# A decode layer pair with its gradients on one core: unread products in TensorE's waits, other staging places, rows issued by SP, one more wq chunk kept

## The chip, the cores and the metric

The kernel runs on one NeuronCore of one Trainium2 chip. The core has five engines with instruction streams of their own: TensorE (PE, matrix products, results only into PSUM), VectorE (DVE), ScalarE (ACT), GpSimd (POOL) and SyncE (SP). SP, ACT and POOL can issue DMA transfers, which all run on the same 16 DMA engines. On chip there are SBUF (128 partitions) and PSUM (8 banks of 128 partitions x 512 fp32). The metric is the device time of one launch in microseconds. Inputs and outputs lie in HBM as the reference has them.

## The reference

One token (a row x of D = 1024 numbers) goes through attention, MLP, attention, MLP, with the same weights both times; then everything is differentiated. In short:

```
A(x): q = x @ wq (1024 -> 32 heads x 128); k, v = the last W = 4096 rows of each of 4 cache heads
      p = softmax(q k^T / sqrt(128)); o = p v; result o @ wo (4096 -> 1024)
B(x): h = x @ w1 + b1 (1024 -> 3584); result (h * tanh(softplus(h))) @ w2 (3584 -> 1024)
x = x + A(layernorm(x)); x = x + B(layernorm(x)); x = x + A(...); x = x + B(...)
outputs: x, and the gradients of x, k_cache, v_cache, wq, wo, w1, b1, w2 for a given grad_out
```

All arrays are bf16. A weight's gradient is the sum over the two layers of an outer product of two vectors, so it is a matrix product over only 2 rows that yields 7.3 to 8.4 MB of output. The cache gradients have 4 heads x 32768 rows x 128; only the last 4096 rows of a head are not zero, so 2 x 29.4 MB of zeros have to be written.

## The kernel before

**Order.** The order of the instructions on every engine is the order in which the Python code emits them; there is no scheduler. The stages follow one another: forward A0, B0, A1, B1 (`attn_fwd`, `mlp_fwd`), backward B1 (`dn_b1`), A1 (`attn_bwd(1, ...)`), the w2 stage (L895 to 900: the second MLP's output and the gradient towards B0's hidden layer), the W1 stage (`dn_b0`, L759), A0 (`attn_bwd(0, ...)`, L1034), and a last stage `work(10000)` (L1042) that finishes the weight gradients.

**Loads.** KT and VS (the used part of the caches, 4 MB each) and W1 stay in SBUF. All chunks of wq, wo and w2 go through a ring of 8 slots of 1 MB (`Ring`, L38). A list of wanted chunks in fixed order (L249 to 265) is worked off by `pump`: whenever a slot is released, SP issues the next load into it. wq is wanted four times (forward and backward of two layers), wo three times (the forward chunks of layer 1 are still in the ring for the backward), w2 twice. `KEEP_Q` (L246) names the wq chunks that layer 0's forward leaves in the ring for layer 1's forward; `KEEP_Q2` (L247) those that layer 1's backward leaves for layer 0's. A kept chunk is not loaded again, and holds its slot meanwhile. In the backward of layer 1 half of every wq chunk is transposed in place; a chunk kept there is not transposed again (`turned_q`).

**Products of one row.** A matrix times one vector is done in two ways side by side. Half of a chunk is multiplied on VectorE (`rowdot`, L392: 1024 columns against the vector, summed). The other half is transposed on PE 128 x 128 at a time into one of three PSUM buffers (`big`), copied back by ACT (`turned`, L417), and then used as the stationary side of products with one column (`mv`, L431), which add up in the PSUM bank TP. `later` (L405) delays these so that PE transposes ahead. A chunk's slot is released after its last product.

**Norms.** `ln_fwd` (L337) and `ln_bwd` (L367) sum over partitions with one small product into the bank SM, which VectorE reads. SM also receives the small sums of the softmax.

**Zeros.** The 56 zero jobs of 1 MB each are issued by POOL in portions: `zeros(n, after)` (L235) first copies one element of `after` on POOL, so that the portion starts when `after` is there, and then issues n jobs. The portions stand at fixed places of the program.

**Weight gradients.** Their outer products need both layers' vectors as rows. `rowize` (L876) and `rowize_f` (L744) transpose a vector's columns on PE, ACT copies the result to SBUF, and two DMAs issued by ACT bring it into `ROWS`. Three of these six run inside `dn_b0`, plus `rowize_f`; two more and the one for GA in the first step of A0's backward (`do1`, L994). One tile of a gradient is a product of 2 rows into 128 x 512 (`unit_dw`, L919), evicted to bf16 by VectorE or ACT, whichever has less work planned (`evac`). Eight tiles (seven for w1) fill one of the staging places in `stage_free`, and SP stores it. Four staging places lie in W1, which is not needed any more after `dn_b0` (L873); in `dq1` (L1010) the eight of VS and KT are put behind them, and for the last stage those of the ring behind these. `work(n)` (L979) emits n tiles, taken in turn from several gradients; it is called between the chunks of A0's backward (`do1`, `dp1`, `dq1`, `dn1`), 53 tiles in all, and then for the remaining 251.

Of the kernel before, what the change touches and what calls it, by code (L numbers as in the profile page):

```python
# [83 lines left out]
def kernel(  # L84
# [62 lines left out]
    SM = psum.tile([P, 512], FP32, name="SM")  # L147
# [98 lines left out]
    KEEP_Q = (6, 7)  # L246
    KEEP_Q2 = (5, 6, 7)  # L247
# [89 lines left out]
    def ln_fwd(x, st, dst_bf, name):  # L337

        nc.tensor.matmul(SM[:, 0:2], lhsT=onesD[:], rhs=st[:], start=True, stop=True)
        mv = tmp([P, 2], FP32, "mv")  # L340
        nc.vector.tensor_copy(mv[:], SM[:, 0:2])
# [12 lines left out]
        nc.scalar.activation(dummy[:, 1:2], dummy[:, 0:1], ACT.Exp)  # L354
        return n32, rstd
# [11 lines left out]
    def ln_bwd(part, n32, rstd, g, name):  # L367
# [12 lines left out]
        nc.tensor.matmul(SM[:, 0:2], lhsT=onesD[:], rhs=st[:], start=True, stop=True)  # L380
        ab = tmp([P, 2], FP32, "ab")
        nc.vector.tensor_copy(ab[:], SM[:, 0:2])
# [19 lines left out]

    lag = deque()
# [46 lines left out]
    def attn_fwd(l, x, st, first, wo_hook, q_hook=None):  # L450
# [19 lines left out]
        nc.gpsimd.tensor_copy(qv[:, 1, :, 1, l, :], qv[:, 0, :, 0, l, :])  # L470
        m64 = [tmp([P, 64], FP32, f"m64{i}") for i in range(2)]
# [20 lines left out]
        nc.tensor.matmul(SM[:, 64:128], lhsT=onesD[0:HQ, :], rhs=dg[:], start=True, stop=True)  # L492
        nm = tmp([P, 64], FP32, "nm")
        nc.vector.tensor_copy(nm[:], SM[:, 64:128])
# [21 lines left out]
        for u in range(2):  # L516
            nc.tensor.matmul(SM[:, 128:160], lhsT=onesD[:], rhs=ssv[:, :, u, :], start=(u == 0), stop=(u == 1))

        rs = tmp([P, HQ], FP32, "rs")
        nc.vector.tensor_scalar(out=rs[:], in0=SM[:, 128:160], scalar1=float(D), scalar2=None, op0=ALU.mult)  # L520
# [178 lines left out]
    def wo_hook1(c):  # L699
        if c == 0:  # L700
            zeros(6, OC[:, 0, 1:2])
# [28 lines left out]
    def dn_b1(g):  # L730
# [11 lines left out]
        return ln_bwd(dnp, sB1["n32"], sB1["rstd"], g, "B1")  # L742

    def rowize_f():  # L744
# [11 lines left out]
    early = [lambda: rowize(OC, HQ, 32, NOFF), lambda: rowize(NA, TD, 0, 0), rowize_f,  # L756
             lambda: rowize(NB, TD, 64, 0), lambda: rowize(AC, TF, 96, NOFF), lambda: rowize(GB, TD, 96, 0)]

    def dn_b0(g):  # L759
        mv_open()  # L760
        for t in range(TD):
            mv(W1[:, t, :], TF, TP[:, t:t + 1], lambda i: DHC[:, i, 0:1], True)
            if t >= 4:
                early.pop()()
        return ln_bwd(None, sB0["n32"], sB0["rstd"], g, "B0")

    def attn_bwd(l, sv, g, wo_key, wq_key, wq_keep, hooks):
# [11 lines left out]
        flush()  # L779
        do_n = from_fours([x.rearrange("p (c k) -> p c k", k=4)[:, :, 2 * h:2 * h + 2]  # L780
# [13 lines left out]
        for i in range(2):  # L794
# [5 lines left out]
            if i == 0:  # L800
                nc.tensor.matmul(SM[:, 192:256], lhsT=onesD[:], rhs=pr[:], start=True, stop=True)
                nc.vector.tensor_copy(sdp[:], SM[:, 192:256])
# [37 lines left out]
        return ln_bwd(dnp, sv["n32"], sv["rstd"], g, name)  # L840
# [35 lines left out]
    def rowize(cols, n, base, off):  # L876
# [6 lines left out]
        for l in range(2):  # L883
            nc.scalar.dma_start(ROWS[base + l:base + l + 1, off:off + n * P].rearrange("o (t p) -> o t p", p=P),  # L884
                                rt[l:2 * n:2, k, :])
# [9 lines left out]
    for c in range(7):  # L895
# [3 lines left out]
        later(lambda c=c: ring.release(("2", 1, c)))  # L899
    flush()  # L900
# [7 lines left out]
    zeros(2, g1)  # L908
# [165 lines left out]
```

## Time and profile before

| what | value |
|---|---|
| time, median of 3 runs | 474.96 us (474.57 to 476.11) |
| profiled execution, its own time | 478.89 us |
| its span | 477.1 us |
| PE busy / DVE busy / ACT busy / POOL busy | 351.7 / 277.9 / 245.3 / 45.2 us |
| mean granted TensorE clock | 0.593 |
| bytes moved by the DMA engines | 183.41 MB, mean 384 GB/s |
| zero jobs on POOL's queue | 56 of 1 MB, 58.7 MB |
| last eviction / end of the span | 457.8 / 477.1 us |

The profile is one execution; times inside it are microseconds from the start of its span, which is 1.8 us shorter than the time of that execution. Busy times of engines overlap and do not add up to the span. A granted clock of 0.5 means that TensorE ran at half speed. The DMA share is the mean busy share of the 16 DMA engines. An entry such as `[1.59 <-DMA W<-W]` behind a row says how long the engine sat idle before it, and what it waited for.

### The profile page before, as it was taken

The numbers are of one execution on the slowest core, as the hardware profiler recorded it, in microseconds if no ns is written. First come the engines' busy times: TensorE is split into PE (matmuls) and PEld (weight loads), VectorE is DVE, ScalarE is ACT, GpSimd is POOL, SyncE is SP. The second block draws the span as 40 slices with busy tenths as digits, with TensorE's granted clock in tenths as the row PEclk, the third lists the DMA queues.
The fourth block names the chain that finished last, engine by engine and source line by source line (L and its number), as shares of the span: only waits on it lengthen the run. The fifth ranks groups of instructions, "written<-read, shape, count | busy, mean of one in ns | idle before, by whom it ended". The sixth has DMA issues, their size and how long they took to land.

```text
span 477.1 us, 13273 instructions
## 1 busy us (share of the span) xinstructions
PE 351.7 (74%) x5841; PEld 268.5 (56%) x5841; DVE 277.9 (58%) x597; ACT 245.3 (51%) x358; POOL 45.2 (9%) x83
## 2 busy tenths in 40 slices
PE   4846345696688895888886976688778689999930
PEld 3746335696588784877876975556456323333300
DVE  4405820561331268896598825466176889999920
ACT  2402001171145296792594633675267589999920
POOL 1000000000043130102201011002302200000000
PEclk9955555555555588797897555555555555555555
DMA  8999999999969999999999999678999999999997
GB/s 337 423 419 419 418 419 418 421 400 383 420 252 394 396 394 406 347 410 368 416 421 366 363 345 414 229 190 325 417 420 415 388 415 413 418 420 414 419 420 306
DMA packets 33992, 183.41 MB, mean 384 GB/s; under 512 B 4217, under 2 KB 4238, under 8 KB 20622
## 3 DMA queue, kind: packets, MB, share of 16 engines
q1 hardware_dynamic: 17280, 123.74, 64.5%
q0 software_dynamic: 15232, 58.72, 31.2%
q8 instruction: 45, 0.74, 0.6%
q10 hardware_dynamic: 1422, 0.10, 0.2%
q14 instruction: 13, 0.11, 0.1%
HBM read 83.90 MB, written 98.58 MB: 382 GB/s over the span
## 4 chain that ended last, share of the span: by engine, by line
PE 46%; DMA 19%; DVE 16%; issue 7%; ACT 6%; ACTq 2%; DVEq 0%; SPq 0%
DVE junk L399 10%; PE BIG L921 8%; PE BIG L421 8%; DMA ring<-in_A_wo_dram 6%; PE SC L921 5%; DMA ring<-in_A_wq_dram 4%; DMA W<-in_B_w_dram 4%; PE BIG L568 3%; ACT ring L282 3%; PE MV L634 3%; DMA out_dram<-W 3%; PE BIG L967 2%; PE TP L433 2%; PE MV L587 2%; ACTq L884 2%
## 5 line engine op out<-in xcount | busy, mean ns | idle before, releaser
L282 ACT COPY ring<-BIG 128x1024 bf16<-128x1024 bf16 x82 | 81.8, 1046 | 38.5 <-PE BIG L421 29.4
L399 DVE CUSTOM_DVE_ANT_0 junk<-ring,SC 128x1024 bf16<-128x1024 bf16 x62 | 75.5, 1217 | 6.1 <-PE SC L305 3.4
L421 PE MATMUL BIG<-ident_bf,ring 128*128 128x128 bf16 x656 | 71.0, 278 | 8.9 <-ACT ring L282 2.4
L921 PE MATMUL BIG<-W 2*128 2x512 bf16 x163 | 68.3, 586 | 7.5 <-ACT W L282 3.2
L421 PEld LDWEIGHTS <-ring 128*128 128x128 bf16 x656 | 57.4, 126 | 22.0 <-issue 21.0
L921 PEld LDWEIGHTS <-W 2*128 2x128 bf16 x240 | 20.2, 101 | 39.9 <-issue 35.3
L243 POOL DMA_DIRECT2D out_dram<-zt x56 | 40.2, 720 | 3.5 <-DMA out_dram<-zt 3.0
L282 ACT COPY KT<-BIG 128x1024 bf16<-128x1024 bf16 x22 | 21.8, 1015 | 31.5 <-PE BIG L568 29.6
L282 ACT CAST W<-BIG 128x512 bf16<-128x512 f32 x55 | 31.2, 595 | 11.5 <-PE BIG L921 9.3
L433 PEld LDWEIGHTS <-ring 128*128 128x128 bf16 x704 | 30.8, 107 | 11.2 <-ACT ring L282 6.3
L921 PE MATMUL SC<-W 2*128 2x512 bf16 x77 | 35.3, 584 | 0.4 <-ACT VS L282 0.4
L282 ACT COPY W<-BIG 128x1024 bf16<-128x1024 bf16 (+2 forms) x33 | 26.5, 908 | 17.2 <-PE BIG L727 14.8
L279 DVE CAST W<-BIG 128x512 bf16<-128x512 f32 x30 | 20.3, 686 | 20.8 <-PE BIG L921 13.4
L539 PE MATMUL MV<-OC,ring 128*128 128x1 bf16 x512 | 16.5, 166 | 13.0 <-DMA ring<-in_A_wo_dram 12.2
L587 PE MATMUL MV<-NB,W 128*128 128x1 bf16 x448 | 16.4, 172 | 10.0 <-DMA W<-in_B_w_dram 6.6
L539 PEld LDWEIGHTS <-ring 128*128 128x128 bf16 x512 | 15.9, 106 | 13.7 <-DMA ring<-in_A_wo_dram 12.8
L461 PE MATMUL MV<-NA,ring 128*128 128x1 bf16 x512 | 15.0, 165 | 10.6 <-DMA ring<-in_A_wq_dram 9.4
L399 DVE CUSTOM_DVE_ANT_0 junk<-ring,DSX 128x1024 bf16<-128x1024 bf16 x18 | 22.0, 1224 | 0.5
L587 PEld LDWEIGHTS <-W 128*128 128x128 bf16 x448 | 16.1, 118 | 10.7 <-DMA W<-in_B_w_dram 7.7
L399 DVE CUSTOM_DVE_ANT_0 junk<-ring,SC,dnp 128x1024 bf16<-128x1024 bf16 x16 | 20.5, 1281 | 0.6
L967 PEld LDWEIGHTS <-W 32*128 32x128 bf16 x128 | 9.6, 101 | 19.9 <-issue 18.3
L461 PEld LDWEIGHTS <-ring 128*128 128x128 bf16 x512 | 14.3, 103 | 11.2 <-DMA ring<-in_A_wq_dram 10.0
(253 smaller groups left out, 593.3 us busy)
## 6 DMA issues: line engine op xcount, KB each, us to landing
out_dram<-zt POOLq DMA_DIRECT2D x56, 1024.0 KB, 13.0
ring<-in_A_wq_dram SPq DMA_DIRECT2D x27, 1024.0 KB
ring<-in_A_wo_dram SPq DMA_DIRECT2D x24, 1024.0 KB
ring<-in_B_w_dram SPq DMA_DIRECT2D x14, 1024.0 KB
out_dram<-W SPq DMA_DIRECT2D x11, 1024.0 KB
W<-in_B_w_dram SPq DMA_DIRECT2D x8, 896.0 KB
out_dram<-KT SPq DMA_DIRECT2D x7, 1024.0 KB
out_dram<-ring SPq DMA_DIRECT2D x7, 1024.0 KB
```

The lines of the kernel that those rows point to most:

```text
L243: nc.gpsimd.dma_start(dst, zt[:, None, :].to_broadcast([P, dst.shape[1], ZC]))
L279: nc.vector.tensor_copy(dst, src)
L282: nc.scalar.copy(dst, src)
L399: nc.vector.tensor_tensor_reduce(out=out, in0=a, in1=vec, scale=1.0, scalar=acc if i else 0.0, op0=ALU.mult, op1=ALU.add, accum_out=acc)
L421: nc.tensor.transpose(b[:, i * P:(i + 1) * P], block(w, i) if block else w[:, i * P:(i + 1) * P], ident_bf[:])
L433: nc.tensor.matmul(out, lhsT=w[:, i * P:(i + 1) * P], rhs=rhs_of(i), start=fresh[0], stop=last and i == n - 1, skip_group_check=True)
L461: nc.tensor.matmul(q_ps[:, h:h + 1], lhsT=ch[:, h * P:(h + 1) * P], rhs=NA[:, t, l:l + 1], start=(t == 0 and h == 0), stop=(t == TD - 1), ...
L539: nc.tensor.matmul(y_ps[:, dd:dd + 1], lhsT=ch[:, tt, dd * P:(dd + 1) * P], rhs=OC[:, h, l:l + 1], start=(h == 0 and dd == 0), stop=(h == ...
L568: nc.tensor.transpose(b[:, i * P:(i + 1) * P], T[:, g, 8 * b8 + i, :], ident_bf[:])
L587: nc.tensor.matmul(h_ps[:, fb:fb + 1], lhsT=f_block(W1[:, t], fb), rhs=NB[:, t, l:l + 1], start=(t == 0 and fb == 0), stop=(t == TD - 1), ...
L921: nc.tensor.matmul(b[:, 0:n], lhsT=ROWS[base:base + 2, lo:lo + P], rhs=ROWS[base:base + 2, ro:ro + n], start=True, stop=True, tile_positio ...
L967: nc.tensor.matmul(b[:, k * 256:(k + 1) * 256], lhsT=RT[32 * g:32 * g + 32, a, tp, :], rhs=YS[32 * g:32 * g + 32, :], start=True, stop=Tru ...
```

## The change

Seven things change together:

1. `warm(n)`: n products of 128 x 512 (the identity as weights, zeros as the moving side) into a PSUM bank WM that nothing reads. 100 of them are emitted: in `from_fours`, before and after the small product of `ln_bwd` (11 and 4 for B1, 8 and 2 for B0, 6 and 4 for A1, none for A0), one per chunk of the w2 stage and of the W1 stage, three at the end of the wo loops, two per chunk of A0's wo and wq loops, six in `dq1`.
2. SM makes room for WM: the small sums go to columns 128 to 384 of TP.
3. `KEEP_Q` gets chunk 5, `KEEP_Q2` chunk 4, so that wq is loaded two chunks less in all.
4. Staging: VS's four places are put in front of the list in `dp1`, KT's four in `dq1`.
5. The row transfers are issued by SP instead of ACT.
6. `rowize_f`, NA and OC are turned to rows right after the norm's product of `ln_bwd` for B0; GB, AC, NB in steps 4 to 6 of the W1 stage; GA stays in `do1`.
7. Zeros: two jobs after the query of layer 1's forward, 5 instead of 6 at wo's first chunk, 3 instead of 2 after g1, two each at c = 2 and c = 5 of A0's wo loop, 4 instead of 5 in `dq1`, 3 instead of 4 at t = 2 of `dn1`; at t = 5 none are left. There are 56 as before.

```diff
-    SM = psum.tile([P, 512], FP32, name="SM")
+    WM = psum.tile([P, 512], FP32, name="WM")
...
-    KEEP_Q = (6, 7)
-    KEEP_Q2 = (5, 6, 7)
+    KEEP_Q = (5, 6, 7)
+    KEEP_Q2 = (4, 5, 6, 7)
...
+        warm(3)
         return TP[:, 480:512]
 
+    def warm(n):
+
+        for _ in range(n):
+            nc.tensor.matmul(WM[:], lhsT=ident_bf[:], rhs=zt[:, 0:512], start=True, stop=True)
...
-    def ln_bwd(part, n32, rstd, g, name):
+    def ln_bwd(part, n32, rstd, g, name, before=0, after=0):
...
-        nc.tensor.matmul(SM[:, 0:2], lhsT=onesD[:], rhs=st[:], start=True, stop=True)
+        warm(before)
+        nc.tensor.matmul(TP[:, 128:130], lhsT=onesD[:], rhs=st[:], start=True, stop=True)
+        while early:
+            early.pop()()
+        warm(after)
         ab = tmp([P, 2], FP32, "ab")
-        nc.vector.tensor_copy(ab[:], SM[:, 0:2])
+        nc.vector.tensor_copy(ab[:], TP[:, 128:130])
...
         nc.gpsimd.tensor_copy(qv[:, 1, :, 1, l, :], qv[:, 0, :, 0, l, :])
+        if not first:
+            zeros(2, QC[:, 0, 8:9])
...
         if c == 0:
-            zeros(6, OC[:, 0, 1:2])
+            zeros(5, OC[:, 0, 1:2])
...
         for l in range(2):
-            nc.scalar.dma_start(ROWS[64 + l:65 + l, NOFF:NOFF + F].rearrange("o (c j) -> o c j", j=512),
+            nc.sync.dma_start(ROWS[64 + l:65 + l, NOFF:NOFF + F].rearrange("o (c j) -> o c j", j=512),
                                 rf[:, 512 * l:512 * l + 512])
...
             mv(W1[:, t, :], TF, TP[:, t:t + 1], lambda i: DHC[:, i, 0:1], True)
-            if t >= 4:
+            warm(1)
+            if t == 4:
+                early.extend(rows)
+            if 4 <= t < 7:
                 early.pop()()
-        return ln_bwd(None, sB0["n32"], sB0["rstd"], g, "B0")
+        return ln_bwd(None, sB0["n32"], sB0["rstd"], g, "B0", 8, 2)
...
         flush()
+        warm(3)
         do_n = from_fours([x.rearrange("p (c k) -> p c k", k=4)[:, :, 2 * h:2 * h + 2]
...
         later(lambda c=c: ring.release(("2", 1, c)))
+        warm(1)
...
+    do1_acc = tmp([P, HQ], FP32, "do32")
+
     def do1(c):
         if c == 0:
             rowize(GA, TD, 32, 0)
-            while early:
-                early.pop()()
             todo[1].append(units_rows(32, HQ, out_5))
...
+        warm(2)
+        if c in (2, 5):
+            zeros(2, do1_acc[:, 4 * c - 4:4 * c - 3])
         if c >= 2:
             work(3)
 
     def dp1():
         zeros(4, tmp([P, 64], FP32, "m641"))
+        stage_free.extendleft(VS[:, g].rearrange("p t d -> p (t d)") for g in range(G))
         work(5)
 
     def dq1():
-
-        for T in (VS, KT):
-            for g in range(G):
-                stage_free.append(T[:, g].rearrange("p t d -> p (t d)"))
+        stage_free.extendleft(KT[:, g].rearrange("p t d -> p (t d)") for g in range(G))
         rowize(DQC, HQ, 0, NOFF)
-        zeros(5, DQC[:, 0, 0:1])
+        zeros(4, DQC[:, 0, 0:1])
+        warm(6)
         work(6)
 
     def dn1(t):
         if t in (2, 5):
-            zeros(4, dnp[:, t:t + 1])
+            zeros(3, dnp[:, t:t + 1])
...
+        warm(2)
         work(3)
```

More of the change, by code (lines that the diff above doesn't have):

```diff
@@ L333, in from_fours @@
             nc.tensor.matmul(TP[:, 480:512], lhsT=spread[:, 3 - k:P + 3 - k], rhs=dm[:, k, :], start=(k == 0), stop=(k == 3))
+        warm(3)
         return TP[:, 480:512]
+    def warm(n):
+        for _ in range(n):
+            nc.tensor.matmul(WM[:], lhsT=ident_bf[:], rhs=zt[:, 0:512], start=True, stop=True)
     def ln_fwd(x, st, dst_bf, name):
-        nc.tensor.matmul(SM[:, 0:2], lhsT=onesD[:], rhs=st[:], start=True, stop=True)
+        nc.tensor.matmul(TP[:, 128:130], lhsT=onesD[:], rhs=st[:], start=True, stop=True)
         mv = tmp([P, 2], FP32, "mv")
-        nc.vector.tensor_copy(mv[:], SM[:, 0:2])
+        nc.vector.tensor_copy(mv[:], TP[:, 128:130])
         nvar = tmp([P, 1], FP32, "nvar")
@@ L379, in ln_bwd @@
                                        accum_out=st[:, 1:2])
-        nc.tensor.matmul(SM[:, 0:2], lhsT=onesD[:], rhs=st[:], start=True, stop=True)
+        warm(before)
+        nc.tensor.matmul(TP[:, 128:130], lhsT=onesD[:], rhs=st[:], start=True, stop=True)
+        while early:
+            early.pop()()
+        warm(after)
         ab = tmp([P, 2], FP32, "ab")
-        nc.vector.tensor_copy(ab[:], SM[:, 0:2])
+        nc.vector.tensor_copy(ab[:], TP[:, 128:130])
         nc.vector.scalar_tensor_tensor(out=t2[:], in0=n32[:], scalar=ab[:, 1:2], in1=dn[:], op0=ALU.mult,
@@ L401, in rowdot @@
         load["D"] += len(vecs) * (n * 1.1e-3 + 0.18)
+    early = []
     lag = deque()
@@ L491, in attn_fwd @@
         nc.vector.tensor_scalar(out=dg[:], in0=id64[:], scalar1=mh[:, 0:1], scalar2=float(D), op0=ALU.mult, op1=ALU.mult)
-        nc.tensor.matmul(SM[:, 64:128], lhsT=onesD[0:HQ, :], rhs=dg[:], start=True, stop=True)
+        nc.tensor.matmul(TP[:, 192:256], lhsT=onesD[0:HQ, :], rhs=dg[:], start=True, stop=True)
         nm = tmp([P, 64], FP32, "nm")
-        nc.vector.tensor_copy(nm[:], SM[:, 64:128])
+        nc.vector.tensor_copy(nm[:], TP[:, 192:256])
         if not first:
@@ L516, in attn_fwd @@
         for u in range(2):
-            nc.tensor.matmul(SM[:, 128:160], lhsT=onesD[:], rhs=ssv[:, :, u, :], start=(u == 0), stop=(u == 1))
+            nc.tensor.matmul(TP[:, 256:288], lhsT=onesD[:], rhs=ssv[:, :, u, :], start=(u == 0), stop=(u == 1))
         rs = tmp([P, HQ], FP32, "rs")
-        nc.vector.tensor_scalar(out=rs[:], in0=SM[:, 128:160], scalar1=float(D), scalar2=None, op0=ALU.mult)
+        nc.vector.tensor_scalar(out=rs[:], in0=TP[:, 256:288], scalar1=float(D), scalar2=None, op0=ALU.mult)
         nc.vector.reciprocal(rs[:], rs[:])
@@ L741, in dn_b1 @@
         flush()
-        return ln_bwd(dnp, sB1["n32"], sB1["rstd"], g, "B1")
+        return ln_bwd(dnp, sB1["n32"], sB1["rstd"], g, "B1", 11, 4)
     def rowize_f():
@@ L752, in rowize_f @@
         for l in range(2):
-            nc.scalar.dma_start(ROWS[64 + l:65 + l, NOFF:NOFF + F].rearrange("o (c j) -> o c j", j=512),
+            nc.sync.dma_start(ROWS[64 + l:65 + l, NOFF:NOFF + F].rearrange("o (c j) -> o c j", j=512),
                                 rf[:, 512 * l:512 * l + 512])
-    early = [lambda: rowize(OC, HQ, 32, NOFF), lambda: rowize(NA, TD, 0, 0), rowize_f,
+    rows = [lambda: rowize(OC, HQ, 32, NOFF), lambda: rowize(NA, TD, 0, 0), rowize_f,
              lambda: rowize(NB, TD, 64, 0), lambda: rowize(AC, TF, 96, NOFF), lambda: rowize(GB, TD, 96, 0)]
@@ L800, in attn_bwd @@
             if i == 0:
-                nc.tensor.matmul(SM[:, 192:256], lhsT=onesD[:], rhs=pr[:], start=True, stop=True)
-                nc.vector.tensor_copy(sdp[:], SM[:, 192:256])
+                nc.tensor.matmul(TP[:, 320:384], lhsT=onesD[:], rhs=pr[:], start=True, stop=True)
+                nc.vector.tensor_copy(sdp[:], TP[:, 320:384])
             s = SC[i].rearrange("p (tp c) -> p tp c", c=64)
@@ L839, in attn_bwd @@
         flush()
-        return ln_bwd(dnp, sv["n32"], sv["rstd"], g, name)
+        return ln_bwd(dnp, sv["n32"], sv["rstd"], g, name, *((6, 4) if l else (0, 0)))
     turned_q = set()
@@ L883, in rowize @@
         for l in range(2):
-            nc.scalar.dma_start(ROWS[base + l:base + l + 1, off:off + n * P].rearrange("o (t p) -> o t p", p=P),
-                                rt[l:2 * n:2, k, :])
+            nc.sync.dma_start(ROWS[base + l:base + l + 1, off:off + n * P].rearrange("o (t p) -> o t p", p=P),
+                              rt[l:2 * n:2, k, :])
     nc.vector.tensor_copy(GB[:, :, 0], g2[:])
@@ L907 @@
     nc.vector.tensor_copy(GA[:, :, 0], g1[:])
-    zeros(2, g1)
+    zeros(3, g1)
     x4 = sb([P, TD], BF16, "x4")
```

## The prediction

> **What bounds the kernel now.** I read the page's slices first, then a table of chosen stretches, then the chain that ended last, then single rows in order of time.
>
> ```profile
> PEclk9955555555555588797897555555555555555555
> DMA  8999999999969999999999999678999999999997
> ```
>
> The DMA engines are busy nearly everywhere and the granted TensorE clock is mostly half. The stretches (PE, PEld, DVE, ACT, POOL busy; then clock, DMA share, GB/s):
>
> ```profile
> 131.00:137.00 6.00, 4.69 (x150) 4.67 (x148) 3.14 (x9) 2.79 (x4) 0.12 (x1) 0.50 0.61 253
> 137.00:150.00 13.00, 12.60 (x301) 12.54 (x301) 1.11 (x2) 6.97 (x7) 4.91 (x7) 0.50 0.87 332
> 190.40:193.80 3.40, 2.15 (x21) 2.06 (x22) 2.03 (x7) 0.12 (x1) 2.19 (x4) 0.50 0.73 298
> 255.00:258.40 3.40, 2.15 (x46) 2.13 (x46) 2.08 (x6) 0.00 (x0) 2.27 (x4) 0.60 0.65 268
> 256.00:281.00 25.00, 22.86 (x473) 22.59 (x474) 17.91 (x33) 14.07 (x14) 2.92 (x6) 0.50 0.96 354
> 281.00:296.00 15.00, 11.14 (x251) 10.00 (x249) 4.13 (x17) 2.08 (x5) 3.34 (x6) 0.50 1.00 383
> 296.00:305.00 9.00, 5.34 (x66) 4.54 (x65) 7.31 (x12) 4.99 (x9) 0.00 (x0) 0.50 0.75 288
> 305.00:328.00 23.00, 18.48 (x195) 12.73 (x196) 12.60 (x22) 18.45 (x27) 0.00 (x0) 0.50 0.71 223
> 384.00:457.80 73.80, 73.00 (x308) 22.59 (x303) 71.17 (x115) 71.61 (x136) 0.00 (x0) 0.50 1.01 417
> 457.80:473.80 16.00, 0.00 (x0) 0.00 (x0) 0.00 (x0) 0.22 (x1) 0.00 (x0) 0.50 1.00 415
> ```
>
> The last two rows decide how everything else counts. The engines finish evicting at 457.8 us (the last store is issued at 458.04), yet the DMA engines stay full for 16 us more: what ends the kernel is the sum of its transfers plus every moment in which the DMA engines had nothing to do. That idle time is 2.3 + 1.7 us at 131 to 150 us, and 2.3 + 6.7 = 9.0 us at 296 to 328 us (length times the share missing from 1); smaller pieces are 0.9 at 190.4 and 1.2 at 255.0. Engine work that ends earlier helps only if it hands transfers over sooner. Why the second hole exists, from the chain of waits:
>
> ```profile
> 289.85 1.18 ACTq L884
> ...
> 301.08 5.00 DMA W<-W
> ...
> 335.47 12.00 DMA out_dram<-W
> ```
>
> and from the rows in order of time:
>
> ```profile
> 306.38 0.82 PE L921 MATMUL BIG<-W 2*128 2x512 bf16 x3 [1.59 <-DMA W<-W]
> ...
> 343.79 0.69 DVE L279 CAST W<-BIG 128x512 bf16<-128x512 f32 x1 [3.99 <-DMA out_dram<-W]
> 347.56 1.29 DVE L279 CAST W<-BIG 128x512 bf16<-128x512 f32 x2 [3.08 <-DMA out_dram<-W]
> ```
>
> ACT spends 286.8 to 302.2 us issuing row transfers; the last lands at 306, and PE, in order, holds its first gradient product (and all behind it) until then. At 343 and 347 VectorE waits for a store to empty one of only four staging slots.
>
> **The change, part by part.** Two sums: the DMA engines', which sets the end, and the engines', which must stay inside the 16 us of slack.
>
> *One more wq chunk kept, twice.* Two loads of 1 MB go. A wq chunk in the stretch of steady loads comes every 2.5 us (PE starts at 24.27, 26.74, 29.23): -5.0 us of transfer. The ring then has one free slot fewer. In the second layer's q stage five loads instead of six go through the same releases, the last still at 110.17 us, so PE gains 0 to 2.5 us; I take 0.7, since after the last landing three kept chunks follow instead of two. In the second case one w2 load moves from before 255 us to after.
>
> *Zeros at other places.* 56 jobs as before (POOL issues each in 0.72 us); 2 go to the second q stage, 4 into the wo loop of layer 0 (c = 2 and 5), 1 more after g1; the last stage loses 4 and others 1 each. The four in the loop are 4.2 MB, 10 us at 417 GB/s, for a hole of 9.0: I take -8.0, bounds 0 (the hole stays) and -9.0. In the first hole 2 go in and 1 goes from the next batch, and one wq load is missing from the stretch: idle there stays about 5; the loads that arrive sooner and the net megabyte give -1.0, bounds 0 and -2.5. At 255 us the chain comes sooner (below) while one load is deferred: -0.8, bounds +1.3 and -1.2. POOL's copies that gate the jobs wait on VectorE; only zeros queue behind them.
>
> *Rate.* 256 to 281 us moves 354 GB/s at a share of 0.96. At 417 it would be 3.8 us shorter, and 281 to 296 us 1.2 (383 GB/s). I take -1.0 between 0 and -5.0, nearer nothing as loads and zeros still mix.
>
> DMA sum: -5.0 - 8.0 - 1.0 - 0.8 - 1.0 = -15.8 us.
>
> *Rows sent by SP.* 16 issues (0.6 to 1.05 us each, 11 us on ACT up to 302) leave ACT. On SP they are queued ahead of the wo loads of chunks 4 to 7; SP is idle then, and chunk 4 is needed some 10 us after chunk 0, so this costs nothing; without that cover up to 11 us. With ACT free, chunks 0 and 1 take about 2 x 2.2 us from 293 and the first product could start near 299 instead of 306: -6.
>
> *Staging first in V's and K's places.* The two waits of 3.99 and 3.08 us go (-7); the six unread products now there cost 1.3 to 2.6: net -5.
>
> *Kept chunk already transposed.* In the last wq loop t = 4 needs no 16 transposes and 2 copies: a period of 2.6 us (that of t = 5 to 7) instead of 3.7: -1.
>
> *100 unread products of 512 columns.* The trace has no such product. Transposes of 128 columns start 0.106 us apart at half clock (16 from 192.58 to 194.28) and 0.055 at full (8 from 201.82 to 202.26); four times that is 0.43 and 0.22 us, so 43 or 22 us on PE in all. The nearest product with 512 columns, L921, shows 0.586 each, which takes the upper bound to 59. I take 0.22 if the clock is granted. What grants it:
>
> ```profile
> 166.60:170.00 3.40, 3.40 (x35) 3.40 (x33) 0.00 (x0) 3.40 (x5) 2.62 (x4) 0.50 1.02 381
> 170.00:173.40 3.40, 3.15 (x54) 2.83 (x51) 2.39 (x7) 3.40 (x5) 1.21 (x2) 0.95 1.02 389
> 183.60:187.00 3.40, 1.84 (x40) 1.42 (x40) 3.26 (x10) 2.65 (x3) 0.00 (x0) 1.00 1.02 402
> 187.40:190.80 3.40, 0.58 (x2) 0.50 (x2) 2.48 (x12) 0.00 (x0) 0.00 (x0) 0.50 1.02 412
> ```
>
> [...] Full clock in the w2 stage: 7 x (16 x 0.051 - 0.22) = -4, VectorE's 2 x 1.25 us per chunk being next; in the wo and wq loops 3.3 instead of 3.7 us per chunk, -2.4 each; layer 1's loops, mostly VectorE-bound, -3. On the path: 8 + 8 products in the W1 stage, 3.5, less 1.6 of transposes moved and waits covered: +1.9. The rest sit in waits for VectorE (3.26 us at 186.6, 1.29 at 253.3); without that cover up to 1.5. [...]
>
> *Small sums move from bank SM to TP.* Same products and copies; PE's order holds them apart: nothing, at most 0.5 us each for the six norms.
>
> Engine sum: -0.7 - 6 - 5 - 1 - 4 - 4.8 - 3 + 1.9 = -22.6: the last stage starts at 361 instead of 384 us. It evicts 251 tiles in 73.8 us and would be done by 435, long before the DMA engines.
>
> The DMA sum is taken from the profiled execution (478.89 us, 1.8 around its span of 477.1), which is 3.9 above the median of 474.96; I subtract it from the median: 459.2 us.
>
> **Rivals.**
> 1. *Rows wait behind loads.* On SP's queue the rows stand behind up to four 1 MB loads, 10 us alone and 20 beside zeros. Against: by then the loads were issued 8 us or more before. For: PE again waits, the 6 us stay. The zeros hang on VectorE's sums, not on rows, so only some 2 us are lost: 461 (460 to 464).
> 2. *Clock stays at half.* The products then cost 0.43 us where nothing covers them: w2 stage 3.0 (PE busy 22.86 of 25), W1 stage 6.2, wo loop 3.8, wq loop 4, the six 2.6, others 1.5: +21 against -14 of removed waits (0.7 + 6 + 7 + 1). The last stage starts at 391, ends at 465; a store lands some 4.5 us later and 3.3 follow: span 473, time 470 (465 to 473). For: the 256.00 row is busy 22.86 of 25 us at 0.50 throughout. [...]
> 3. *Slower: half clock with little cover.* If more than 26 us of the 43 land on the path, the removed waits and 11.5 us of slack (16 less a last store's 4.5) are used up, and beyond that each microsecond counts: at 32, 480 us; at all 43, 491. For: PE is the busiest engine from 256 to 370. Against: PE idles 4.5 us of 23 in the wo loop.
> 4. *Better.* The rate term comes to 5 and every hole closes: 452 (448 to 454).
>
> **How the numbers follow.** Forecast 0.57 (454 to 464, its own range), rival 1 0.07, rival 2 0.14, rival 4 0.07, rival 3 0.10, and 0.05 for landing within 0.3% (1.4 us, about what a measurement of this kernel tells from no change). Faster: 0.57 + 0.07 + 0.14 + 0.07 = 0.85. The range, 452 to 473, leaves out rival 3, no change and about half of rival 4: 0.10 + 0.05 + 0.035, near 0.2.
>
> **What would show it.** DMA packets fall by two wq loads (27 to 25); the share from 296 to 328 us rises from 0.7 to over 0.9; no wait for out_dram<-W or W<-W in the chain before the last stage; PEclk near 1.0 through the w2, wo and wq stages; the last stage starting 15 to 25 us sooner, with the DMA engines still full after the last eviction. The forecast is wrong if the last eviction sets the end, if the clock row shows 0.5 after 256 us, or if the hole only moves, say to the time before g3 or to the W1 stage.

## The result, and the profile after

The changed kernel takes 480.67 us (median of 4 runs, 479.06 to 482.62), the kernel before 475.53 us beside it (474.57 to 476.58): a ratio of 1.0109, 95% interval 1.0064 to 1.0155. It is 5.1 us slower, where 459.2 was predicted (452 to 473).

The profiled execution took 480.4 us with a span of 478.6. The slices of the page:

```profile
PEclk9955555555555599997888756855665955555555
DMA  8999999999999999999995997989999949999997
```

The clock is above half in most slices from the 15th to the 32nd, where before it was at half from the 23rd on. The DMA engines' 6 at 131 us is gone, and 6, 7 and 8 at 299 to 335 have become 9, 8, 9. Three others stand in their place: a 5 at 251 to 263 us, a 7 at 287 to 299 and a 4 at 383 to 395. The stretches (PE, PEld, DVE, ACT, POOL busy; then clock, DMA share, GB/s):

```profile
131.00:137.00 6.00, 4.71 (x135) 4.52 (x133) 3.58 (x7) 3.58 (x5) 0.00 (x0) 0.50 1.02 426
251.60:255.00 3.40, 3.40 (x19) 1.68 (x18) 1.79 (x9) 0.33 (x1) 0.00 (x0) 0.58 0.05 19
256.00:281.00 25.00, 20.04 (x457) 18.37 (x455) 17.20 (x28) 13.86 (x14) 1.67 (x3) 0.76 0.93 340
281.94:297.20 15.26, 15.26 (x256) 9.94 (x256) 1.26 (x9) 1.07 (x4) 2.19 (x4) 0.52 0.89 335
296.00:305.00 9.00, 7.56 (x108) 5.53 (x108) 7.83 (x19) 7.00 (x10) 3.94 (x7) 0.97 0.72 279
305.00:328.00 23.00, 11.41 (x112) 7.68 (x112) 9.37 (x16) 9.60 (x14) 1.61 (x3) 0.54 0.94 344
380.80:394.40 13.60, 9.57 (x70) 3.49 (x69) 11.12 (x27) 8.66 (x18) 0.00 (x0) 0.54 0.47 189
394.40:463.90 69.50, 68.84 (x289) 21.35 (x286) 66.78 (x109) 67.43 (x128) 0.00 (x0) 0.50 1.01 417
463.90:475.40 11.50, 0.00 (x0) 0.00 (x0) 0.00 (x0) 0.00 (x0) 0.00 (x0) 0.50 1.00 414
```

The hole at 131 us is closed, where the prediction left about 5 us of idle time there, and the one at 305 to 328 nearly so, while 296 to 305 stays at 0.72. But 13.6 x 0.53 = 7.2 us of idle DMA engines are new at 381 to 394, and 3.2 at 251.6 to 255. The last stage starts near 390 us, not at 361 and not even at 384. The rows of TensorE in order of time say what it did instead:

```profile
269.91 1.01 PE L647 MATMUL MV<-AC,ring 128*128 128x1 bf16 x32 [4.46 <-DMA ring<-in_B_w_dram]
291.89 4.00 PE L340 MATMUL WM<-zt,ident_bf 128*128 128x512 bf16 x9
313.79 0.82 PE L939 MATMUL BIG<-W 2*128 2x512 bf16 x3 [10.10 <-DMA W<-W]
```

At full clock (1.00 from 255.6 to 269.2 us) TensorE runs into a w2 load that has not landed. Nine unread products stand in a row ahead of the norm of the W1 stage, at half clock (0.50 from 269.2 to 296.5 us), 4 us on the path. And the first gradient product waits 10.10 us for a row, where it waited 1.59 before. The rows of SP beside it:

```profile
288.49 6.19 SPq L901 DMA_DIRECT2D W<-W  x6
297.93 2.23 SPq L766 DMA_DIRECT2D W<-W  x2
300.27 8.10 SPq L901 DMA_DIRECT2D W<-W  x6
308.48 13.59 SPq L68 DMA_DIRECT2D ring<-in_A_wo_dram  x4
```

SP needs until 308.4 us to issue the rows, and the load of wo chunk 4 comes behind them, at 308.48.

Milestones, in us from the start of each profiled execution (the start of the VectorE instruction that makes the value), with two kernels of the experiments:

| | before | changed | without unread (e2) | split rows (e10) |
|---|---|---|---|---|
| g3, layer 1's MLP norm | 191.3 | 189.3 | 191.1 | 187.5 |
| DOC, layer 1 | 218.1 | 214.6 | 217.9 | 212.8 |
| g2, layer 1's attention norm | 255.8 | 255.1 | 255.5 | 252.5 |
| dh0, end of the w2 stage | 280.1 | 281.5 | 281.1 | 275.6 |
| g1, end of the W1 stage | 291.7 | 296.9 | 291.7 | 285.0 |
| first gradient product | 306.4 | 313.8 | 309.5 | 296.8 |
| DOC, layer 0 | 328.4 | 339.6 | 332.6 | 319.3 |
| g0; the last stage follows | 382.7 | 388.3 | 380.7 | 369.5 |
| last eviction starts | 457.4 | 463.3 | 455.7 | 444.6 |
| span | 477.1 | 478.6 | 471.0 | 460.0 |
| from g0 to the end of the span | 94.4 | 90.3 | 90.3 | 90.5 |
| idle DMA engines in all | 20.8 | 26.7 | 21.2 | 12.8 |

The last row adds, over stretches of 3.4 us from 2.0 us on, the length times the share missing from 1, less what lies beyond the span. (Stretches that begin elsewhere give totals some 2 us higher, and differences of 5 to 6 us between the first two columns.) With it a span is a sum: before, 20.8 idle and 456.3 in which 183.41 MB went at 402 GB/s; changed, 26.7 idle and 451.9 in which 181.33 MB went at 401. The two loads were saved (4.4 us less of transfer) and 5.9 us of new idle time more than ate them. These two spans lie only 1.5 us apart, the medians 5.1.

The experiments ran in four groups (e1 to e4, e5 to e8, e9 to e12, e13 to e16), each with the kernel before on the same chip, at medians of 477.46, 477.48, 478.20 and 477.64 us. The first number of each result is the ratio to that, with its 95% interval; differences between kernels are taken from the ratios, in us at 477.

### The profile page after: what moved, and what is told of

Same layout as the page of the kernel before. It is cut to its first block, busy times and chain, and to the rows that moved or that the text cites. A ratio compares the mean times of both kernels' runs of the same rounds, so it can differ in the third digit from the quotient of the medians.

```text
span 478.6 us, 13442 instructions
## 1 busy us (share of the span) xinstructions
PE 363.2 (76%) x5925; PEld 263.6 (55%) x5925; DVE 276.1 (58%) x595; ACT 244.5 (51%) x358; POOL 45.6 (10%) x85
## 2 busy tenths in 40 slices
DMA packets 33705, 181.33 MB, mean 379 GB/s; under 512 B 4185, under 2 KB 4206, under 8 KB 20590
## 5 line engine op out<-in xcount | busy, mean ns | idle before, releaser
L282 ACT COPY ring<-BIG 128x1024 bf16<-128x1024 bf16 x80 | 79.5, 1047 | 33.9 <-PE BIG L432 23.7
L939 PE MATMUL BIG<-W 2*128 2x512 bf16 x164 | 62.7, 568 | 13.0 <-DMA W<-W 10.1
L432 PE MATMUL BIG<-ident_bf,ring 128*128 128x128 bf16 x640 | 61.6, 256 | 10.3 <-ACT W L282 4.0
L432 PEld LDWEIGHTS <-ring 128*128 128x128 bf16 x640 | 50.3, 115 | 17.9 <-issue 17.4
L243 POOL DMA_DIRECT2D out_dram<-zt x56 | 40.3, 722 | 3.9 <-DMA out_dram<-zt 3.3
L340 PE MATMUL WM<-zt,ident_bf 128*128 128x512 bf16 x100 | 39.7, 507 | 0.0
L444 PEld LDWEIGHTS <-ring 128*128 128x128 bf16 x704 | 29.3, 104 | 8.0 <-ACT ring L282 4.4
L282 ACT CAST W<-BIG 128x512 bf16<-128x512 f32 x36 | 20.1, 591 | 22.7 <-PE BIG L939 20.7
L279 DVE CAST W<-BIG 128x512 bf16<-128x512 f32 x25 | 16.8, 685 | 17.9 <-PE BIG L939 17.5
L552 PEld LDWEIGHTS <-ring 128*128 128x128 bf16 x512 | 15.9, 106 | 14.4 <-DMA ring<-in_A_wo_dram 13.9
L600 PEld LDWEIGHTS <-W 128*128 128x128 bf16 x448 | 15.9, 118 | 10.9 <-DMA W<-in_B_w_dram 8.2
L985 PE MATMUL BIG<-W 32*128 32x256 bf16 x80 | 20.0, 381 | 0.5 <-ACT ring L282 0.5
## 6 DMA issues: line engine op xcount, KB each, us to landing
out_dram<-zt POOLq DMA_DIRECT2D x56, 1024.0 KB, 12.7
```

The source lines that it names most:

```text
L243: nc.gpsimd.dma_start(dst, zt[:, None, :].to_broadcast([P, dst.shape[1], ZC]))
L279: nc.vector.tensor_copy(dst, src)
L282: nc.scalar.copy(dst, src)
L340: nc.tensor.matmul(WM[:], lhsT=ident_bf[:], rhs=zt[:, 0:512], start=True, stop=True)
L432: nc.tensor.transpose(b[:, i * P:(i + 1) * P], block(w, i) if block else w[:, i * P:(i + 1) * P], ident_bf[:])
L444: nc.tensor.matmul(out, lhsT=w[:, i * P:(i + 1) * P], rhs=rhs_of(i), start=fresh[0], stop=last and i == n - 1, skip_group_check=True)
```

## The experiments: the change, one part undone at a time

**e1: ACT issues the rows again.**

```diff
-            nc.sync.dma_start(ROWS[base + l:base + l + 1, ...
+            nc.scalar.dma_start(ROWS[base + l:base + l + 1, ...
(and so for the pair in rowize_f)
```

> The changed kernel with one part undone: ACT issues the row transfers again. Theory (rows on SP's queue stand behind one another and ahead of the wo load of chunk 4, so that the first gradient product waits 10.10 us and the load is issued only at 308.48 us): the wait for W<-W falls under 4 us, the first load of chunk 4 is issued by 302, the last evictions end 6 to 10 us sooner than 463.9, and the time falls from 480.7 to 471 to 475. Rival (the unread products at half clock and the shorter ring cost the time, and the rows' wait is covered by work that has to wait anyway): the first product may come sooner, but the time stays within 2 us of the changed kernel, 479 to 482.

Measured: 1.0101 (1.0065 to 1.0137), 481.97 us: no difference. The first product does not start sooner but at 316.69 us, behind a wait of 3.65 instead of 10.10. ACT now spends 1.3 to 2.7 us on each pair of issues until 310.2 us, and its copies of transposes, without which TensorE can't go on, stand behind them. The time has the rival's value: beside the unread products it makes no difference which engine issues.

**e2: no unread products.**

```diff
-        for _ in range(n):
+        for _ in range(0):
             nc.tensor.matmul(WM[:], ...
```

> The changed kernel without its 100 unread products, all else kept (nothing that is read is left out). Theory (they hold the clock only in short stretches and lie on the path where it is at half: some 15 us on TensorE between 281 and 390 us): the last stage starts 5 to 10 us sooner than about 390, the time falls to 472 to 476. Rival (the full clock that they buy before 269 and at 296 to 306 us is worth what they cost): 479 to 482, with the W1 stage shorter and the w2 stage longer by about as much.

Measured: 0.9880 (0.9845 to 0.9915), 472.47 us, as the theory had it. The products cost 1.0109 - 0.9880 = 2.3% or 10.9 us; without them the rest of the change is a gain. g1 comes at 291.7 instead of 296.9, g0 at 380.7 instead of 388.3. The wait for the last row stays:

```profile
309.50 0.82 PE L939 MATMUL BIG<-W 2*128 2x512 bf16 x3 [10.63 <-DMA W<-W]
```

**e3: two and three kept chunks, as before.**

```diff
-    KEEP_Q = (5, 6, 7)
-    KEEP_Q2 = (4, 5, 6, 7)
+    KEEP_Q = (6, 7)
+    KEEP_Q2 = (5, 6, 7)
```

> The changed kernel with as many kept wq chunks as before (two and three instead of three and four, so two loads of 1 MB more). Theory (four kept chunks leave four free slots at 248 us, hence 5.7 us of idle DMA engines there, the stop of 3.6 us for a w2 load at 266 us, and 2.7 us at 92 to 112): these idle stretches go, some 7 us, the two loads cost 5.0, and the w2 stage ends 3 to 4 us sooner, so that the time falls by 2 to 5 us, to 476 to 479. Rival (the sum of transfers sets the end, as the prediction had it): 5 us longer, 485.

Measured: 1.0040 (1.0008 to 1.0071), 479.51 us. Two loads more, and not 5 us longer but, by the ratios, 0.7% shorter than the changed kernel. The intervals overlap a little; e9, e8 with e4, and e14 ask it again.

**e4: all three undone**, so staging, zeros, earlier turning of rows and the small sums' bank are left.

> All three undone together: what is left of the change is the staging order, the zeros' places, the earlier turning of the rows and the small sums in the other bank. Theory (each of the three costs time, in different places): faster than the kernel before, by the 7 us of staging waits and a filled hole: 466 to 472. Rival (staging and zeros bring nothing, since the end is the sum of transfers and the last stage's evictions): within 1.5 us of before, 474 to 477.

Measured: 0.9958 (0.9939 to 0.9977), 475.70 us. The time is the rival's: of the 8 us forecast for the zeros and of the staging waits together, 2 us arrive.

## The experiments: which unread products

**e5: without the 18 of the W1 stage.**

```diff
             mv(W1[:, t, :], TF, TP[:, t:t + 1], lambda i: DHC[:, i, 0:1], True)
-            warm(1)
...
-        return ln_bwd(None, sB0["n32"], sB0["rstd"], g, "B0", 8, 2)
+        return ln_bwd(None, sB0["n32"], sB0["rstd"], g, "B0")
```

> The changed kernel without the 18 unread products of the W1 stage (one behind each of the eight t, eight before the norm and two behind it), the other 82 kept. Theory (each costs about 0.43 us at half clock on the path: g1 came at 291.7 us without any unread products and at 296.9 with them, and a last stage that starts later makes the end later by as much): g1 near 292 us, the time 4 to 6 us under the changed kernel, a ratio to before near 1.000. Rival (TensorE only waits elsewhere for the same time, for the rows or the loads): under 2 us gained, ratio 1.007 to 1.011.

Measured: 1.0002 (0.9970 to 1.0035), 477.27 us: 1.07% or 5.1 us of the 10.9 lie in these 18 products. The theory held, with its number.

**e6: only the 31 of layer 1** (e5, and the calls `warm` in the w2, wo, dq and wq places of layer 0 taken out).

> The changed kernel with only the 31 unread products of layer 1 (11 and 4, 6 and 4 at its two norms, 3 and 3 before its small sum), none from 256 us on. Theory (what layer 1 gains up to 230 us is lost by 255 us, where the loads that the shorter ring holds back and a cold clock take it back, so these products are worth about nothing, and all of the cost lies after 281 us): the ratio to before 0.985 to 0.990, as without any. Rival (layer 1's products pay: 2 to 3 us sooner at every milestone): 0.980 to 0.984. Other rival (they too cost): 0.992 or more.

Measured: 0.9843 (0.9787 to 0.9899), 469.65 us. Against e2 (0.9880) the intervals overlap; against e5 it is 1.6% or 7.6 us, which is what the 51 products of the w2, wo, dq and wq places of layer 0 cost. So the sum of the 69 from 256 us on is 12.7 us, and layer 1's 31 give back some of it.

## The experiments: rows, and the load behind them

**e7: e2, with the products that need the last row from chunk 4 on.**

```diff
             rowize(GA, TD, 32, 0)
-            todo[1].append(units_rows(32, HQ, out_5))
         if c == 4:
+            todo[1].append(units_rows(32, HQ, out_5))
```

> The kernel without unread products, in which the products that need the last row (that of g1's columns) join the queue of work at chunk 4 of the wo loop instead of chunk 0; same products, same stores, another order. Theory (TensorE, in order, waits 10.6 us with its first gradient product for the row that is issued last): that wait falls below 4 us, the last stage starts 4 to 8 us sooner than 382, and the time falls by 3 to 7 us below 472.5. Rival (the wo load of chunk 4, issued behind the rows, comes late by itself): the wait moves to the chunk, and the time stays within 1.5 us.

Measured: 0.9901 (0.9869 to 0.9933), 473.04 us: nothing gained. My theory fell, and the rival's mechanism is there to read on TensorE:

```profile
300.57 0.64 PE L939 MATMUL BIG<-W 2*128 2x512 bf16 x3 [1.18 <-DMA W<-W]
313.54 1.03 PE L432 MATMUL BIG<-ident_bf,ring 128*128 128x128 bf16 x8 [8.52 <-DMA ring<-in_A_wo_dram]
```

The first product starts 9 us sooner, and then chunk 4 is missing, whose load SP issues at 303.62 us behind the rows. Before, the first load in this loop is that of chunk 5: with four kept wq chunks only four of the eight slots hold wo chunks, with three kept five.

**e8: e2 with rows by ACT.**

> The kernel without unread products, with ACT issuing the rows again (kept chunks, staging and zeros as changed). Theory (the queue makes little difference, as it made none beside the unread products: the transfers take their time on either, and the first product waits for the last of them): within 1.5 us of the 472.5 with SP, ratio 0.986 to 0.991. Rival (SP's issue frees ACT for copies, worth some 3 us): 0.992 to 0.996, about that of the kernel with the kept chunks undone as well (0.9958).

Measured: 0.9992 (0.9966 to 1.0019), 477.14 us: SP is worth 1.1% or 5.3 us here, against my theory, and more than the rival gave it. In this profile the wo loop is hardly slower (g1 to DOC: 289.2 to 331.3 us, 42.1; in e2 40.9). The larger difference lies behind it, from DQC to g0: 41.1 us against 36.2. (The two profiled executions are only 2.4 us apart in span, 473.4 and 471.0, so they hold less than half of the difference.) On ACT at that place:

```profile
344.92 5.29 ACTq L901 DMA_DIRECT2D W<-W  x2
350.25 0.59 ACT L282 CAST W<-BIG 128x512 bf16<-128x512 f32 x1 [5.36 <-DMA W<-W]
```

The last of the eight pairs of rows, that of DQC, holds ACT for 5.29 us, in a slice of the page with a DMA share of 0.9 or more, and the evictions wait behind it. In e2 SP issues it in 1.96 us, with only a store behind it. In e1 the same pair took 2.08 us, so the size varies. Why SP gains nothing over ACT beside the unread products is not shown: from DQC to g0 e1 takes 40.3 us and the changed kernel 37.7, from g1 to DOC 41.9 and 42.7.

**e9: e2 with the kept chunks of before.**

> The kernel without unread products and with the kept chunks as before (two and three, so two loads of 1 MB more); rows by SP, staging and zeros as changed. Theory (the shorter ring costs more in late loads than the two loads save: beside the unread products the undoing gave 0.7%, though ACT's rows beside both undone gave only 0.3%): a ratio to before of 0.980 to 0.986, 1 to 4 us under the 0.988 with the kept chunks. Rival (without the unread products the late loads are covered, and the two loads' 5 us of transfer count): 0.992 to 0.998.

Measured: 0.9840 (0.9807 to 0.9872), 471.14 us: 0.4% better than e2 with 2 MB more to load; inside the theory's range, the rival's is excluded, but the intervals of e2 and e9 overlap.

**e10: rows on both queues.** Layer 1's unread products (e6), kept chunks of before, e7's order, and:

```diff
-            nc.sync.dma_start(ROWS[base + l:base + l + 1, ...
+            (nc.sync if l else nc.scalar).dma_start(ROWS[base + l:base + l + 1, ...
```

> Layer 1's unread products only, kept chunks as before, the products that need the last row from chunk 4 on, and of each pair of rows one issued by ACT and one by SP. Theory (on one queue the row issues take some 16 us and hold up either the products or the load of chunk 4, which waited 8.5 us when only the order was changed; on two queues they take half): no wait over 4 us for rows or loads in the wo loop, the last stage starts near 376, ratio 0.970 to 0.978. Rival (the transfers, not the issuing, take the time beside the zeros): the wait of 8 us stays at one of the two places, ratio 0.980 to 0.986.

Measured: 0.9666 (0.9633 to 0.9698), 462.24 us, the best of all: 16 us under the kernel before on the same chip, and a little better than the theory's 0.970 to 0.978. TensorE waits for no row and no load in the wo loop. The stretches:

```profile
280.00:352.00 72.00, 60.45 (x816) 44.40 (x816) 43.71 (x85) 41.61 (x63) 14.12 (x25) 0.50 1.02 413
365.80:376.00 10.20, 5.95 (x29) 2.04 (x30) 7.82 (x21) 4.96 (x11) 0.00 (x0) 0.50 0.50 206
371.00:445.00 74.00, 72.78 (x307) 22.24 (x303) 71.04 (x115) 71.52 (x136) 0.00 (x0) 0.50 0.98 403
445.00:457.00 12.00, 0.00 (x0) 0.00 (x0) 0.00 (x0) 0.16 (x1) 0.00 (x0) 0.50 1.01 419
```

Here much of the prediction's picture is real: no hole from 280 to 352 us, and full DMA engines for 12 us after the last eviction. But 10.2 x 0.50 = 5.1 us of idle DMA engines stand at 365.8 to 376, just ahead of the last stage's stores: in this kernel too a part of the hole has moved there.

**e13 and e16: e10 with all rows by SP, and e10 with the products in the old order.**

> The kernel with split rows (0.9666), all rows by SP again, the order of the products kept. Theory (SP's row issues hold back the load of chunk 4, so TensorE waits some 8 us for it): ratio 0.978 to 0.986. Rival (the order alone gives the gain here): 0.965 to 0.970.

> The kernel with split rows, the products that need the last row in the queue of work from chunk 0 on again. Theory (on two queues the last row is issued by about 295 us instead of 303, so the first product waits some 3 us instead of 10): ratio 0.968 to 0.974. Rival (the wait for the last row stays as long): 0.978 or more.

Measured: e13 0.9693 (0.9669 to 0.9717), e16 0.9731 (0.9694 to 0.9769). In e13 the rival was right: with the order changed, one queue is nearly as good as two (the intervals of e13 and e10 overlap). On TensorE:

```profile
293.83 0.61 PE L939 MATMUL BIG<-W 2*128 2x512 bf16 x3 [1.65 <-DMA W<-W]
307.43 1.03 PE L433 MATMUL BIG<-ident_bf,ring 128*128 128x128 bf16 x8 [3.75 <-DMA ring<-in_A_wo_dram]
```

The order that gained nothing in e7 seems to gain in e13, where the load behind the rows is chunk 5's and not chunk 4's: 3.75 us of waiting and not 8.52. That ties the size of the wait in the wo loop to the kept chunk. The gain itself is an estimate, since no run has e13 in the old order: e9 (0.9840) less layer 1's 0.6% (below) would be near 0.978. Without the order but with both queues (e16) the first product waits 3.20 us for the last row, as the theory had it; the intervals of e16 and e10 just overlap.

## The experiments: the parts alone, and the kept chunk again

**e11: before, with staging first in V's and K's places.**

```diff
     def dp1():
         zeros(4, tmp([P, 64], FP32, "m641"))
+        stage_free.extendleft(VS[:, g].rearrange("p t d -> p (t d)") for g in range(G))
...
-        for T in (VS, KT):
-            for g in range(G):
-                stage_free.append(T[:, g].rearrange("p t d -> p (t d)"))
+        stage_free.extendleft(KT[:, g].rearrange("p t d -> p (t d)") for g in range(G))
```

> The kernel before with one part of the change alone: staging first in V's and K's places. Prediction's step: the waits of 3.99 and 3.08 us go, the last stage starts some 5 to 7 us sooner, but the DMA engines' sum stays, so the time does not change by more than 1 us. Theory now (what the DMA engines still hold when the last stage starts is only what was queued in time, so an earlier last stage is worth most of its microseconds): 2 to 5 us faster, ratio 0.990 to 0.996.

Measured: 0.9989 (0.9969 to 1.0009). The prediction's step holds, my later theory does not: the last stage starts 3 us sooner, and full DMA engines after it take the 3 us back.

```profile
381.00:454.80 73.80, 72.80 (x307) 22.51 (x303) 70.98 (x115) 71.69 (x136) 0.00 (x0) 0.50 1.01 418
454.80:470.00 15.20, 0.00 (x0) 0.00 (x0) 0.00 (x0) 0.01 (x1) 0.00 (x0) 0.50 1.01 421
```

**e12: before, with the zeros' places of the change** (the calls of `zeros` alone).

> The kernel before with one part of the change alone: zeros at other places. Prediction's step: the hole at 296 to 328 us is filled, -8 us and -1, ratio 0.980 to 0.983. Theory now (the zeros that fill the hole are missing before the last stage, at 380 to 395 us, so the hole only moves, and the rows and loads of the wo loop land later beside them): within 2 us of before, ratio 0.996 to 1.004, with idle DMA engines of 5 us or more between 370 and 395.

Measured: 0.9984 (0.9964 to 1.0003). The 8 us do not come. The profiled execution (span 474.2) shows where they go:

```profile
296.00:305.00 9.00, 3.65 (x48) 3.23 (x47) 3.24 (x6) 3.67 (x6) 0.00 (x0) 0.50 1.02 402
305.00:328.00 23.00, 17.43 (x179) 12.21 (x179) 11.97 (x20) 16.84 (x25) 1.61 (x3) 0.50 0.83 287
373.00:395.00 22.00, 16.21 (x126) 6.01 (x125) 19.15 (x38) 14.86 (x30) 0.00 (x0) 0.50 0.55 225
```

The hole of 9.0 us is 3.9, and 22 x 0.45 = 9.9 us of idle time stand at 373 to 395. Before, POOL issued its last four zeros from 375.87 us on, just ahead of the last stage; here the last is issued at 362.4, and nothing is queued until the last stage's stores are ready. Beside the zeros the wo loop itself is slower: from g1 to DOC 42.2 us instead of 36.7. ACT's row issues after g1 take 2.0 to 2.6 us a pair in place of 1.2 to 1.6, and TensorE waits 3.40 us for the last row instead of 1.59. How much of the 5.5 us these carry was not measured.

**e14 and e15: e10 with the kept chunks of the change, and e10 without unread products.**

> The kernel with split rows and the kept chunks as in the change (three and four, two loads of 1 MB fewer). Prediction's step (the sum of the transfers sets the end, which the profile of the kernel with split rows shows with full DMA engines for 15 us after the last eviction): -5 us, ratio 0.954 to 0.960. Rival (the ring with one free slot fewer leaves DMA engines idle at 92 to 112 and 248 to 258 us, for as long as is saved): 0.964 to 0.972.

> The kernel with split rows, without any unread products. Theory (layer 1's 31 bring some 3 us on TensorE up to 230 us, of which the end sees at most a part): ratio 0.966 to 0.972, no more than 2.5 us above the 0.9666 with them. Rival (they are worth nothing, since the DMA engines set the end): 0.963 to 0.968; other rival (all of the 3 us arrive): 0.973.

Measured: e14 0.9779 (0.9755 to 0.9804), e15 0.9727 (0.9700 to 0.9753). With everything else early and the DMA engines full at the end, one more kept chunk still makes the kernel 1.1% or 5.4 us slower, outside both expectations. Its stretches and its row of TensorE:

```profile
92.00:112.00 20.00, 17.74 (x394) 17.49 (x394) 15.14 (x40) 12.86 (x14) 0.00 (x0) 0.50 0.85 315
248.00:260.00 12.00, 10.83 (x182) 8.11 (x182) 9.40 (x22) 6.09 (x8) 2.32 (x4) 0.86 0.60 241
```

```profile
270.67 1.01 PE L648 MATMUL MV<-AC,ring 128*128 128x1 bf16 x32 [6.00 <-DMA ring<-in_B_w_dram]
```

In e10 the same stretches have shares of 0.99 and 0.79: the shorter ring adds 2.8 and 2.3 us of idle DMA engines, which is the two loads' 5.0 again. Layer 1's MLP norm (g3) comes at 191.1 us instead of 187.5; the loads that were asked for late then hold TensorE for 6.00 us at 270 and 2.89 at 311, and g0 comes at 375.2 instead of 369.5, 5.7 us later. The span is 5.8 us longer. In all four pairs that differ in this alone the kept chunk costs (e3 and the changed kernel 0.7%, e9 and e2 0.4%, e4 and e8 0.3%, e10 and e14 1.1%); only in the last do the intervals stay apart.

Layer 1's 31 unread products are worth 0.6% or 2.9 us between e15 and e10 (the intervals only just stay apart: 0.9698 and 0.9700). That is the whole of the 3 us that the prediction gave them, a little more than this run's theory allowed, though with these intervals it may be 1 us or 5.

## Why the prediction was wrong, point by point

**What bounds the kernel.** As a sum, "what ends the kernel is the sum of its transfers plus every moment in which the DMA engines had nothing to do" holds in every profile. That the engines have "16 us of slack" inside it is the step that failed. The end follows g0, after which the last stage starts: before, the span ends 94.4 us after g0, and in the changed kernel and the 15 others with the zeros' new places it ends 89.4 to 90.6 us after g0, though their spans go from 460.0 to 480.2. In the changed kernel and in e10, whose rows are shown above, the DMA engines have run out of work just ahead of the last stage's stores (7.2 us idle at 381 to 394, 5.1 at 366 to 376), and in this state each microsecond of g0 is one at the end, to within 0.6 us in these 16 profiles. The exception is e11, which keeps the zeros' old places: g0 comes 3.2 us sooner (379.5) and the span stays at 477.1.

Full DMA engines after the last eviction do not show slack: they were full for 11.5 and 12 us in these two kernels as well. By estimate the last stage's 251 tiles of 0.131 MB are 32.9 MB, which is 79 us at 417 GB/s, and the engines evict them in about 74; with the first stores moving only from about 394 us in the changed kernel, some 4 us after its last stage starts, most of that rest arises within the stage. What the queues held at g0 beyond it was, by the same comparison, worth 94.4 less 90, some 4 us; the four zeros issued at 375.87 us (4.2 MB, 10 us at 417 GB/s) stood in them. So the slack was some 4 us and not 16, and moving those zeros forward spent it. The engines' sum, -22.6, then decided, and it came out with the other sign: g0 is 5.6 us later (388.3 after 382.7).

**Zeros: -8.0.** Alone they gave nothing that stands clear of noise (e12): the span's end moves from 94.4 to 89.7 us after g0, and g0 comes 1.8 us later. The hole was filled and another opened ahead of the last stage, in e10 too. And the term had a cost that I put at nothing, the rows and loads beside which the zeros run. Of the two terms of -1.0, the first hole gave more than forecast (it closed), and the rate nothing: 256 to 281 us moved 340 GB/s, after 354 before.

**One more wq chunk kept: -5.0.** This is the first step that failed by its own mechanism. Fewer bytes, but a ring with one slot fewer asks for its loads later, and where the end follows g0 fewer bytes bring nothing by themselves; I priced that slot at "0 to 2.5" of gain, and at 1.3 at worst at 255 us. The runs price it as a loss of 1.6 to 5.4 us in all. The step "t = 4 needs no 16 transposes and 2 copies: -1" was right and too small: from DQC to g0, e2 takes 36.2 us and e9 39.4, e14 36.4 and e10 39.6.

**Rows sent by SP: -6.** The step said "SP is idle then, and chunk 4 is needed some 10 us after chunk 0, so this costs nothing; without that cover up to 11 us". It was the cover that was gone: 14 of the 16 issues take SP until 308.4 us, the last row makes the first product wait 10.10 us, so that it starts at 313.8 and not near 299, and chunk 4's load stands behind. I had priced the issues at 0.6 to 1.05 us, as on ACT in the kernel before (DMA share 1.02 from 286.75 to 297 us, 0.68 from 296 to 302); on SP they took 1.0 to 1.4 each with what they wait for (share 0.87 from 288.49 to 308.4), and they had to wait for ACT's copies too. What SP did bring, 5.3 us in e8 against e2, was at a place that I did not name.

**Staging: -5.** The waits went and the last stage starts 3 us sooner in e11: the mechanism was right, the size 3.

**100 unread products.** Predicted -9.9 on the engines (w2 -4, wo and wq -4.8, layer 1 -3, W1 +1.9), measured +10.9 us of time. Layer 1's -3 is right (2.9). In the W1 stage 5.1 were measured where 1.9 stood. I had 16 of its 18 products on the path at the price of full clock, 0.22, less 1.6 of waits covered; the clock was at half there (0.50 up to 296.5 us), and 16 x 0.43 less 1.6 is 5.3. In the w2 stage the clock did rise, to 0.92 to 1.00 up to 265 us, and the gain of 4 is nil, since TensorE then waits for w2 loads: from g2 to dh0 it takes 26.4 us with the products and 25.6 without (e2) with four kept chunks, 24.2 with (e3) and 23.5 without (e9) with three. In the wo loop the clock rose by 297 us and fell again in the wait for the row; from then on two unread products per chunk cost 0.9 us at half clock (by estimate, from the nine that took 4.00), the condition that rival 2 named.

That full clock would be granted in the w2, wo and wq stages, on which the terms of -4 and -4.8 rest, was my estimate, and no run shows these terms. What raises the clock is not settled by the rows that the prediction shows: in the kernel before TensorE was busy for all of 259.1 to 265.9 us, and the clock was 0.50 throughout. In the changed kernel it was 1.00 from 255.6 to 269.2 us, 0.50 from there to 296.5, 1.00 to 306.7, 0.50 through the rest of the wo loop (306.8 to 339.6), and 0.66 in the mean from 344.4 to 388. In the waits that start at 265.4 us (4.46) and at 303.7 us (10.10) it goes from 1.00 to 0.50.

**The rivals.** Rival 3, "half clock with little cover", had the right sign and, by its own price list, the right size (480). But its mechanism carries 10.9 us, not 32, so the size is luck; the rest of the distance to 459 is gains that did not come. The 4.5 us for a last store, in rivals 2 and 3, was an estimate that no run shows: in the kernel before the quickest store of zeros landed 4.8 us after its issue. Rival 1's wait appeared turned around: the rows did not stand behind the loads, a load stood behind the rows. That is the sort of pair that I should have costed together, a shorter ring and a longer queue ahead of its first load.

**What would show it.** Of the marks listed, loads of wq 27 to 25, the share of 0.94 at 305 to 328 us (but 0.72 from 296 to 305), and no wait for out_dram<-W came as written; W<-W stayed in the chain, the clock was full only in parts, and the last stage came 6 us later instead of 15 to 25 sooner. The DMA engines were full after the last eviction, as written, but that mark shows no slack. The last sentence of that part, "or if the hole only moves", is what happened.

**What stays open.** Why one kept chunk costs 0.3 to 0.7% in three pairs and 1.1% in the fourth is not settled (in the fourth, 3.6 of the 5.7 us stand at g3 already), nor what made one pair of issues take 5.29 us in e8, nor why SP gains nothing beside the unread products. The engines' work from g1 to the last stage was not separated further.

## What to carry to other kernels

Full DMA engines between the last instruction and the end (here 11.5 and 12 us) are no slack to spend: look whether the queues run empty before the last stage. If they do, the end follows the start of that stage (here 89.4 to 90.6 us after g0), and bytes saved or holes filled earlier count only as far as they bring that start forward. Keeping data in a ring saves its load and takes a slot (here two loads of 1 MB saved, 0.3 to 1.1% lost), so price the slot at every later place where the ring is short, and at the transfers that will stand ahead of its first load on the issuing queue. Products that nobody reads paid here where TensorE waits for another engine (layer 1's norms: 2.9 us; the clock, at 0.50 from 187.4 to 197.6 us before, was 1.00 from 166.8 to 218.0), and cost their full half-clock time where they stand ahead of a norm (5.1 us in the W1 stage) or where the clock fell in the next wait for a transfer (1.00 to 0.50 in the wait of 10.10 us).

## What was not expected of the hardware

TensorE was busy for all of 281.94 to 297.20 us, and the granted clock was 0.50 up to 296.5 us: through stretches of 28 one-column products with a single product of 512 columns between them, and through nine products of 512 columns in a row (291.89, 4.00 us). From 296.5 us on it was 1.00; which of these products raised it was not tested. And an issue of a row transfer of 2 to 8 KB is not a fixed price: a pair of them took 1.16 to 1.35 us on ACT beside a DMA share of 0.68 (before, 296 to 302 us), 1.3 to 2.8 beside a share of 1.02 (e4, 282 to 298 us), and once 5.29 (e8, 344.92 us).
